# Zero products in the idle time of the TensorE queue, and a planner with another clock and fetch model: a fused delta-rule attention and two MLPs on one Trainium2 core

## The chip, the cores and the metric

The kernel runs on one core of one Trainium2 chip. The metric is the device time of one execution in microseconds (us), the median of several runs. Five queues matter: PE (TensorE), ACT (ScalarE), DVE (VectorE), POOL (GpSimd) and SP (which issues the DMAs). Each executes its own instructions in the order in which they were emitted and waits on semaphores for the others.

## What is computed

```python
k_n = k / (norm(k) + 1e-6)
for t in range(768):                       # 4 batches x 8 heads, head size 48
    y[t]  = q[t] @ state
    state = state + beta[t] * outer(k_n[t], v[t] - k_n[t] @ state)
x = y as [3072, 384]
x = ((x @ w_a) * (x @ w_b)) @ w_out        # hidden size 1536
h = x @ w_in                               # hidden size 2048
out = (max(h, 0) + alpha * min(h, 0)) @ w_out2
```

All tensors are float32.

## The kernel before

The sequence is cut into six pieces of 128 steps (`c = 0..5`), each of two halves of 64 (`j`). For a piece the kernel forms products of the keys with the keys and with the queries (`gram_keys`, `gram_queries`, PSUM tiles `g`), masks them (`ef` on DVE, `Z` on POOL), inverts the triangular 32x32 blocks by a chain of small DVE operations (`inverting`: pairs `itmp`, `inv`), transposes the result (`diagonal`: `hw`, `TT` on DVE), joins the blocks (`offdiag`: products `w`, ACT copies into `hw`, products `xx`, ACT copies into `TT`), and then walks through the two halves (`step`: products `rp`, `up`, `sp`, `yp`, with `v` and `SU` evicted between them). `columns` splits `yp` into the high and the low float32r half of `x`. All products of this part are fp32 with at most 128 columns, and the profile shows two PE instructions for each.

The MLPs use float32r products of 128x128 by 128x512, three for each fp32 product (high by high, low by high, high by low). The first MLP has, for a piece, 12 hidden blocks `m` of nine products `p` for `w_a`, nine `p` for `w_b` and nine `o` for `w_out`. Its weights come packed. `decode` unpacks each by ACT (`W`, `e`), DVE (two operations on `raw`) and POOL (`W`); `prepare` splits it into a ring `u` of four tiles `wu` by ACT and POOL. The order in which weights are prepared is fixed: `w_a` and `w_b` of block 0, of block 1, `w_out` of block 0, `w_a` and `w_b` of block 2, `w_out` of block 1, and so on. The second MLP (products `h` and `o`) follows when all six pieces are through the first.

"The front" is what comes ahead of the first `p` of piece 0. In it the core loads pieces 0 and 1 (called `L` and `N` in the code), does the whole attention of piece 0, and does `N`'s products of keys and queries and `N`'s inversion beside it. The inversions of `L` and `N` run in a PSUM tile `inv` of a pool `p0`, which also has the bank `g`. The bank for the products `o` comes from a pool that begins only when `p0` is no longer used (`Pool(rec, second, (p0,), 1, True)`), thus after `N`'s inversion and the two transposes that read it. The other PSUM banks of the front are rings by tag: `chain` (two banks: two of `L`'s query products, then `w`, `xx`, `rp`, ...), `ab` (two), `pre` (one).

Nothing of this is emitted in program order. A `Recorder` takes all operations down with what they depend on; `Recorder.link` adds the dependences that come from tiles sharing a place; `Schedule` groups consecutive small products into one task, gives each task a cost, computes its level (the longest chain of work behind it, in which the large products also follow one another), and `Schedule.run` plays the whole kernel through: always the engine that can begin first, and on it the ready task of the highest level. The order of the starts is the order of emission on each queue. In this play a product costs double while a small model of PE's clock says slow. The model of before starts fast, adds up PE's busy time in steps of fixed length, and switches by two shares, `RISE` and `KEEP_UP`.

Of the kernel before, what the change touches and what calls it, by code (L numbers as in the profile page):

```python
# [6 lines left out]
F32R = mybir.dt.float32r  # L7
# [11 lines left out]
class View:  # L19
# [3 lines left out]
    def __init__(s, tile, path, p, ix):  # L23
        s.tile, s.path, s.p, s.ix = tile, path, p, ix
# [101 lines left out]
PE_, ACT_, DVE_, POOL_, SP_ = range(5)  # L126


class Recorder:
# [35 lines left out]

    def link(s):

        for pool in s.pools:
            earlier = {n for p in pool.after for r in p.rooms for n in r.uses}
            rings = {}  # L170
            for room in sorted((r for r in pool.rooms if r.uses), key=lambda r: r.uses[0]):
                ring = rings.setdefault(room.kw.get("tag", id(room)), [])
                first = s.ops[room.uses[0]]
                for n in earlier:
                    first.before.setdefault(n, 0)
                k = room.kw.get("bufs", pool.bufs)
                if len(ring) >= k:
                    for n in ring[-k].uses:
                        first.before.setdefault(n, 0)
                if ring:  # L180
                    first.before.setdefault(ring[-1].uses[0], 1)
                for n in room.uses[1:]:
                    s.ops[n].before.setdefault(first.n, 1)
                ring.append(room)
        for op in s.ops:
            op.before.pop(op.n, None)
# [17 lines left out]
HOP, SAME = 0.15, 0.03  # L204
ENTER, LEAVE = 0.2, 0.19
SLACKS = (0.25, 0.15, 0.15, 0.3, 0.3)
WINDOW, RISE, KEEP_UP = 3.413, 0.93, 0.66


class Task:  # L210
# [4 lines left out]
def large(op):  # L215
    return op.name == "matmul" and op.dst.ix.size >= 256
# [6 lines left out]
class Schedule:  # L223

    def __init__(s, rec):
        s.tasks, s.of = [], {}
        for op in rec.ops:
            t = s.tasks[-1] if s.tasks else None
            if op.eng == PE_ and not large(op) and t and t.eng == PE_ and not t.large and t.ops[-1].n == op.n - 1:
                t.ops.append(op)  # L230
            else:
                t = Task()
                t.n, t.eng, t.ops, t.large = len(s.tasks), op.eng, [op], op.eng == PE_ and large(op)
                t.port, t.dma, t.after, t.rows = False, op.name == "dma_start", [], None
                s.tasks.append(t)
            s.of[op.n] = t.n
        for t in s.tasks:
            s.costs(t)
            t.before = {}
            for op in t.ops:  # L240
                for n, kind in op.before.items():
                    m = s.of[n]
                    if m != t.n:
                        t.before[m] = min(kind, t.before.get(m, 1))
            for m in t.before:
                s.tasks[m].after.append(t.n)

    def costs(s, t):
        op, k = t.ops[0], len(t.ops)
# [67 lines left out]
    def run(s, level):  # L317

        tasks = s.tasks
        waits = [len(t.before) for t in tasks]  # L320
        ready, start, end = ([0.0] * len(tasks) for _ in range(3))
        open_ = [[t.n for t in tasks if t.eng == e and not waits[t.n]] for e in range(5)]
        free, port, link, was = [0.0] * 5, 0.0, 0.0, False
        rows = [None] * 5
        landed, order = [], []
        clock = {"w": 0, "busy": 0.0, "fast": True}

        def fast(b):
            while (clock["w"] + 1) * WINDOW <= b:
                share = clock["busy"] / WINDOW  # L330
                clock["fast"] = share >= (KEEP_UP if clock["fast"] else RISE)
                clock["busy"], clock["w"] = max(0.0, clock["busy"] - WINDOW), clock["w"] + 1
                if clock["busy"] == 0 and (clock["w"] + 1) * WINDOW <= b:
                    clock["fast"] = False
            return clock["fast"]

        while len(order) < len(tasks):
            at, e = min((min(max(ready[n], free[e]) for n in open_[e]), e) for e in range(5) if open_[e])
            n = max((n for n in open_[e] if ready[n] <= at + SLACKS[e]), key=lambda n: (level[n], -n))
            open_[e].remove(n)  # L340
            t = tasks[n]
            order.append(n)
            b = max(ready[n], free[e])
            cost, lag = t.cost, t.lag
            if e in (ACT_, DVE_, POOL_):
                if rows[e] == t.rows:
                    b = max(ready[n], free[e] - (0.12 if e != DVE_ else 0.1))
                rows[e] = t.rows
            if t.port:
                wait = max(0.0, port - b - 0.1)  # L350
                port = b + wait + t.lag - 0.05
                cost, lag = cost + wait, lag + wait
            if e == PE_:
                if t.large == was:
                    b += ENTER if not t.large else LEAVE
                    clock["busy"] += 0.2
                was = not t.large
                if not fast(b):
                    cost *= 2
                    lag = lag + t.cost  # L360
                clock["busy"] += cost
            if t.dma:
                if e == SP_:
                    if len(landed) >= 8:
                        b = max(b, landed[-8])
                    landed.append(0)
                link = max(b + 1.5, link) + lag
                end[n] = link + 0.55
                if e == SP_:
                    landed[-1] = end[n]  # L370
            else:
                end[n] = b + lag
            start[n] = b
            free[e] = b + cost
            for m in t.after:
                u = tasks[m]
                if u.before[n]:
                    r = b + 1e-6
                elif u.eng == e == PE_:
                    r = b + cost  # L380
                else:
                    r = end[n] + (SAME if u.eng == e and not t.dma else HOP)
                ready[m] = max(ready[m], r)
                waits[m] -= 1
                if not waits[m]:
                    open_[u.eng].append(m)
        s.start, s.end = start, end
        return sorted(order, key=lambda n: (start[n], n))


B, H, S, D = 4, 8, 768, 48
# [57 lines left out]
def f32(ap):  # L449
    return ap.bitcast(F32)  # L450
# [415 lines left out]
def attn_moe_kernel(tc, kt, qt, kn, vn, beta, w_a, w_b, w_o, w_in, w_o2, alpha, out):  # L866
    nc = tc.nc
    with ExitStack() as ctx:
        ctx.enter_context(tc.manual_schedule(engines={getattr(mybir.EngineType, e) for e in ("PE", "Activation", "DVE", "Pool", "SP")}))
        rec = Recorder(nc)  # L870
        nc = rec

        def pool(name, stack=ctx, bufs=1, **k):
            p = Pool(rec, None, (), bufs, k.get("space") == PSUM)
            p.real = stack.enter_context(tc.tile_pool(name=name, bufs=bufs, **k))
            return p

        cp, wp, xp, gp = pool("const"), pool("wp"), pool("xp"), pool("gp", bufs=2)
# [12 lines left out]
        def bank(name, tag):  # L891
            return pools[tag].tile([128, 512], F32, tag=tag, name=name, bufs=BANKS[tag])
# [29 lines left out]
        now, until = 0.0, {ACT: 0.0, DVE: 0.0, POOL: 0.0, SP: 0.0}  # L922
# [182 lines left out]
        def finish(b):  # L1105
            for _ in b:
                pass
            background[:] = [x for x in background if x is not b]
# [13 lines left out]
        A.masks(L, 1, xroom(0, 1, [16, 64], F32, "mb1"))  # L1122
        A.scale_values(L, 0)
        A.clear()

        ef1 = wp.tile([128, 32, 64], F32, tag="late", name="ef1")
        for jg, tag in zip(HALF, ("ab", "ab", "g", "pre")):
# [12 lines left out]
        A.scale_values(L, 1)  # L1140
        norms = A.norms(N, ef1, late=True)
        next(norms)
        keys = [A.gram_keys(N, *jg, tag) for jg, tag in zip(HALF, ("g", "pre", "ab", "ab"))]
        finish(inv)
        finish(A.diagonal(L))
        finish(norms)
# [67 lines left out]
        free, spare = ["mb", "eu", "ef"], [f"w{n}" for n in range(6)]  # L1214
# [49 lines left out]
        now = 220.0  # L1264
# [15 lines left out]
        n = 0  # L1280
# [17 lines left out]
        for c in range(NSC):  # L1298
# [3 lines left out]
            if c > 0:  # L1302
                N = A.load(c + 1) if c + 1 < NSC else None
                if c == 1:
                    finish(inv)
                    diagonal = A.diagonal(L)
                    now = max(now, until[DVE])
# [9 lines left out]
                tag = "chain" if c == 1 else "pre"  # L1317
# [48 lines left out]
        def fetched(c):  # L1366

            fs = []
            for kk in range(KT):
                fs.append(wp.tile([128, 512], F32, tag=("w6", "w8", "w9")[kk], name="xf"))  # L1370
                nc.sync.dma_start(fs[kk], x2d[c][kk])
            return fs
# [56 lines left out]
        first = hidden2(0, xn)  # L1429
# [4 lines left out]
        for c in range(NSC):  # L1434
            xs = xn
            for m in range(M2):
                if m == XAT and c + 1 < NSC:
                    xf, xn = fetched(c + 1), []
                if c == m == 0:
                    g = first  # L1440
                elif c == NSC - 1 and m == M2 - 1:
                    g = hidden2(m, xs, 2, nc.vector)
                else:
                    g = hidden2(m, xs)
# [4 lines left out]
                if m == 0:  # L1449
                    o = [bank("o2", tag) for tag in OUT[c % 2]]  # L1450
# [1 line left out]
        down2(*todo)  # L1452
        rec.link()
        plan = Schedule(rec)
        rec.emit([op.n for n in plan.run(plan.levels()) for op in plan.tasks[n].ops])


def _layout(q, k, v, beta, moe_w_a, moe_w_b, moe_w_out, moe2_w_in, moe2_w_out, moe2_alpha):
# [74 lines left out]
```

## Time and profile before

| | |
|---|---|
| three runs | 1020.69, 1021.53, 1021.54 us; median 1021.53 us |
| profiled execution, first to last instruction (span) | 1019.1 us |
| what lies around the span, against the median | 2.4 us |
| PE busy | 977.5 us (96%), 9950 products |
| DVE, POOL, ACT busy | 610.0, 574.7, 477.4 us |
| PE busy from 100 to 200 us | 99.93 of 100 us |
| PE busy in the first 80 us | 45.07 of 80 us |
| granted clock of PE, mean of the span | 0.977 |

The time of the profiled execution itself isn't listed beside its span; the table sets the span against the median of the three runs. [...] In the profile PE is busy nearly without a break from the first `p` at 81.04 us to the end of the last product at about 1013.8 us; before that its work is small, with gaps, and the clock rises and falls. So the page as a whole says that PE is the bound, and the front has to be read for itself, engine by engine.

### The profile page before, as it was taken

What the parts mean: (1) busy time and instruction counts of PE and PEld (TensorE: products, weight loads), DVE (VectorE), ACT (ScalarE), POOL (GpSimd) and SP (SyncE); (2) the same over time, 40 slices, a digit from 0 to 9 for tenths busy, and PEclk for the clock granted to TensorE, in tenths of its full rate; (3) what the DMA queues carried; (4) which work ended last, traced back from release to release, by engine and by line L of the source; (5) the groups of instructions that cost most, each with busy time, mean ns of one, the idle gap of its engine ahead of it and who ended that gap; (6) DMA issues with size and microseconds to landing.
All of it is one profiled execution on the core that took longest, in us unless ns stands there. A gap on an engine that the chain in (4) does not pass through costs nothing.

```text
span 1019.1 us, 23984 instructions
## 1 busy us (share of the span) xinstructions
PE 977.5 (96%) x9950; PEld 805.1 (79%) x9950; DVE 610.0 (60%) x1232; ACT 477.4 (47%) x955; POOL 574.7 (56%) x512
## 2 busy tenths in 40 slices
PE   6279999999999999999999999999999999999998
PEld 5267877888888788878878888888888888888886
DVE  6999667854783587368648899543343443433333
ACT  5477875565547455645578886122121221211211
POOL 7668998667567566755546996333333333333332
PEclk9569999999999999999999999999999999999999
DMA  9624434101300220000025541101020020000000
GB/s 248 190 81 126 138 115 132 40 2 50 110 1 8 74 79 1 18 19 32 17 64 171 178 146 50 32 19 44 1 63 0 1 63 1 32 1 1 32 0 32
DMA packets 26940, 61.41 MB, mean 60 GB/s; under 512 B 4304, under 2 KB 8912, under 8 KB 26832
## 3 DMA queue, kind: packets, MB, share of 16 engines
q1 hardware_dynamic: 26400, 59.50, 19.3%
q8 instruction: 78, 1.28, 0.5%
q10 hardware_dynamic: 432, 0.39, 0.1%
q14 instruction: 30, 0.25, 0.1%
HBM read 50.44 MB, written 9.44 MB: 59 GB/s over the span
## 4 chain that ended last, share of the span: by engine, by line
PE 91%; DVE 5%; ACT 1%; issue 1%; DMA 1%; SPq 0%; DVEq 0%; POOL 0%; ACTq 0%
PE o L201 34%; PE p L201 29%; PE h L201 19%; PE up L201 2%; PE yp L201 2%; PE g L201 2%; DVE itmp L201 1%; DVE inv L201 1%; PE rp L201 1%; PE sp L201 1%; DMA k<-in_kn_dram 1%; PE xx L201 1%; PE w L201 1%; DVE raw L201 1%; DVE ef L201 0%
## 5 line engine op out<-in xcount | busy, mean ns | idle before, releaser
L201 PE MATMUL p<-x,wu 128*128 128x512 f32 x1296 | 318.0, 394 | 1.4 <-DVE x L201 0.7
L201 PEld LDWEIGHTS p<-x,wu 128*128 128x128 f32 x1296 | 240.2, 188 | 56.2 <-issue 2.4
L201 POOL TENSOR_TENSOR g<-neg,g 128x512 fp32r<-128x512 f32 x95 | 124.3, 1308 | 256.2 <-ACT g L201 255.6
L201 POOL TENSOR_TENSOR wu<-W,wu 128x384 fp32r<-128x384 f32 x195 | 200.3, 1033 | 110.6 <-ACT wu L201 109.0
L201 PE MATMUL h<-x,v 128*128 128x512 f32 x864 | 211.4, 389 | 0.0
L201 PE MATMUL o<-g,v 128*128 128x512 f32 x870 | 211.4, 388 | 0.0
L201 DVE TENSOR_SCALAR neg<-h,al 128x512 f32<-128x512 f32 (+1 forms) x97 | 72.2, 745 | 218.3 <-PE h L201 218.3
L201 ACT CAST g<-neg 128x512 fp32r<-128x512 f32 (+1 forms) x97 | 59.7, 616 | 298.8 <-DVE neg L201 277.3
L201 PEld LDWEIGHTS o<-g,v 128*128 128x128 f32 x870 | 162.5, 188 | 33.4
L201 PEld LDWEIGHTS h<-x,v 128*128 128x128 f32 x864 | 162.2, 188 | 33.7
L201 PE MATMUL o<-g,wu 128*128 128x512 f32 x648 | 165.5, 394 | 0.5 <-DVE TT L201 0.5
L201 ACT CAST wu<-W 128x384 fp32r<-128x384 f32 x216 | 109.9, 513 | 78.7 <-PE p L201 38.2
L201 PEld LDWEIGHTS o<-g,wu 128*128 128x128 f32 x648 | 120.0, 188 | 27.1 <-issue 0.9
L201 POOL TENSOR_TENSOR g<-a,g 128x512 fp32r<-128x512 f32 x71 | 93.3, 1314 | 30.3 <-ACT g L201 30.1
L201 PE MATMUL g<-Z 48*64 48x64 f32 (+1 forms) x1024 | 66.4, 275 | 27.9 <-DVE ef L201 17.9
L201 DVE TENSOR_TENSOR a<-p,a 128x512 f32<-128x512 f32 x72 | 49.3, 685 | 49.8 <-PE p L201 22.4
L201 DVE TENSOR_TENSOR inv<-inv,itmp 128x240 f32<-128x240 f32 (+23 forms) x236 | 69.9, 296 | 10.4 <-ACT eu L201 2.8
L201 PEld LDWEIGHTS g<-Z 48*64 48x64 f32 x1024 | 50.6, 160 | 28.9 <-DVE ef L201 18.2
L201 DVE SCALAR_TENSOR_TENSOR neg<-h,neg 128x512 f32<-128x512 f32 (+1 forms) x97 | 66.5, 686 | 3.3
L201 ACT COPY a<-p 128x512 f32<-128x512 f32 x72 | 42.2, 586 | 44.7 <-PE p L201 41.6
L201 ACT CAST g<-a 128x512 fp32r<-128x512 f32 x72 | 44.7, 620 | 22.5 <-DVE a L201 22.0
L201 POOL TENSOR_TENSOR f<-f,v 128x384 int32<-128x384 int32 x32 | 38.2, 1205 | 6.6 <-DVE v L201 4.0
(87 smaller groups left out, 948.5 us busy)
## 6 DMA issues: line engine op xcount, KB each, us to landing
v<-in_w_o_dram SPq DMA_DIRECT2D x16, 384.0 KB, 3.2
v<-in_w_in_dram SPq DMA_DIRECT2D x16, 384.0 KB, 3.7
k<-in_kn_dram SPq DMA_DIRECT2D x6, 768.0 KB, 4.6
Z<-in_kt_dram SPq DMA_DIRECT2D x24, 192.0 KB, 4.4
Z<-in_qt_dram SPq DMA_DIRECT2D x24, 192.0 KB, 4.0
raw<-in_w_a_dram SPq DMA_DIRECT2D x12, 384.0 KB, 4.0
v<-in_vn_dram SPq DMA_DIRECT2D x12, 384.0 KB, 3.3
raw<-in_w_b_dram SPq DMA_DIRECT2D x12, 384.0 KB, 4.4
```

Of the source, the lines that this page charges most:

```text
L201: getattr(s.engines[op.eng], op.name)(*(real(x) for x in op.a), **{w: real(x) for w, x in op.k.items()})
```

## The change

- A tile `still` of 128x512 zeros is made by a memset on DVE. It uses the ring `a`, which the first MLP uses later.
- `spins` records 120 products of `still` with itself (128x128 by 128x512, float32r) into a bank, under a tag. There are two such groups: `early`, into the ring `chain` between `L`'s second query product and `w`; and `late`, into the bank `g` behind `N`'s first key product. Nothing reads what they write.
- `Schedule` takes tagged operations out of the tasks. In `run`, ahead of each PE task until the first large product, `spin` fills the time from when PE is free until `REST` (0.5 us) before the task's planned start with as many of these products as fit, at 0.227 us each or double while the clock model says slow. `early` stops when the first task that needs its bank (`w`) has begun, and gives it at least one product; `late` goes on until the first large product. Products that don't fit are not emitted.
- The clock model starts slow, keeps a list of PE's busy stretches instead of one sum, counts the zero products as busy, and has other constants.
- A model of PE's instruction stream is new: a stock of instructions, then pieces of 256, each asked for when the piece before it is begun and there 3.5 us later, or 6.6 us while data is being loaded. A PE task is planned longer by the wait for a piece.
- The order in which the tasks are emitted follows from this play, so it may differ from that of before on every queue, SP's and POOL's included. No data product, DMA or vector operation is added or left out but the memset and the zero products.

```diff
+        s.next = {}
...
+                    s.next.setdefault(ring[-1].uses[0], []).append(first.n)
...
-WINDOW, RISE, KEEP_UP = 3.413, 0.93, 0.66
+REST, SPIN, SPINS = 0.5, 0.227, 120
+CHUNK, STOCK, FETCH_IDLE, FETCH_BUSY = 256, 446, 3.5, 6.6
+WINDOW, RISE, KEEP_UP = 3.413, 0.98, 0.65
...
+            if op.tag is not None:
+                spins.setdefault(op.tag, []).append(op)
+                continue
...
+        s.spins = []
+        for ops in spins.values():
+            ends = [s.of[n] for n in rec.next.get(ops[0].n, ())]
+            s.spins.append((ops, [s.of[n] for n in ops[0].before], ends))
...
-        clock = {"w": 0, "busy": 0.0, "fast": True}
+        spins, filled = [0] * len(s.spins), []
+        chunk, spans = {"at": 0, "next": 0.0}, []
+        clock = {"w": 0, "fast": False}
...
+        def ask(b):
+            chunk["next"] = b + (FETCH_BUSY if link > b + 1 else FETCH_IDLE)
+
+        def fetched(b, cost, n):
+            at, late = chunk["at"], 0.0
+            for x in range(at, at + n):
+                if x == STOCK - CHUNK:
+                    ask(b)
+                if x >= STOCK and (x - STOCK) % CHUNK == 0:
+                    now = b + late + cost * (x - at) / n
+                    late += max(0.0, chunk["next"] - now)
+                    ask(max(now, chunk["next"]))
+            chunk["at"] = at + n
+            return late
+
+        def spin(b, t):
+            for g, (ops, before, ends) in enumerate(s.spins):
+                if all(end[n] for n in before) and not any(end[n] for n in ends):
+                    at = max(free[PE_], max(end[n] for n in before) + HOP)
+                    while spins[g] < len(ops):
+                        each = SPIN if fast(at) else 2 * SPIN
+                        if at + each > b - REST and (spins[g] or t.n not in ends):
+                            break
+                        filled.append((at, 0, ops[spins[g]]))
+                        spins[g] += 1
+                        spans.append((at, at + each))
+                        fetched(at, each, 2)
+                        at += each
+                    b = max(b, at)
+            return b
...
             if e == PE_:
+                if not done:
+                    b = spin(b, t)
+                done = done or t.large
...
+                late = fetched(b, cost, 2 if t.large else 4 * len(t.ops))
+                cost, lag = cost + late, lag + late
+                spans.append((b, b + cost))
...
+        still = gp.tile([128, 512], F32R, tag="a", name="still")
+        nc.vector.memset(f32(still), 0.0)
+
+        def spins(name, tag):
+            rec.now_tag, o = name, bank(name, tag)
+            for _ in range(SPINS):
+                nc.tensor.matmul(o, still[:, 0:128], still, start=True, stop=True)
+            rec.now_tag = None
...
+        spins("early", "chain")
         keys = [A.gram_keys(N, *jg, tag) for jg, tag in zip(HALF, ("g", "pre", "ab", "ab"))]
+        spins("late", "g")
```

## Rows read from the trace of the kernel before

**Rows 1.** The page: each engine's busy time, share of the span, instructions.
```profile
PE 977.5 (96%) x9950; PEld 805.1 (79%) x9950; DVE 610.0 (60%) x1232; ACT 477.4 (47%) x955; POOL 574.7 (56%) x512
```

**Rows 2.** Busy time by stretch: length, PE, PEld, DVE, ACT, POOL, clock, DMA, GB/s.
```profile
40.00:60.00 20.00, 11.08 (x384) 10.23 (x384) 18.71 (x45) 14.98 (x30) 6.54 (x6) 0.50 0.10 33
60.00:80.00 20.00, 17.03 (x569) 16.23 (x571) 18.84 (x46) 12.98 (x30) 15.05 (x14) 0.72 0.38 102
```

**Rows 3.** Single microseconds, PE alone: length, busy (products), clock, DMA, GB/s.
```profile
12.00:13.00 1.00, 1.00 (x24) 1.00 1.06 212
16.00:17.00 1.00, 1.00 (x42) 1.00 1.00 205
46.00:47.00 1.00, 1.00 (x25) 0.50 0.00 0
64.00:65.00 1.00, 1.00 (x34) 0.75 0.10 16
71.00:72.00 1.00, 0.00 (x0) 0.66 0.28 52
```

**Rows 4.** PE in order of time, the front: start, length, what [idle before].
```profile
26.88 1.27 PE L201 MATMUL g<-Z 48*64 48x64 f32 x35 [1.33 <-issue]
44.84 3.75 PE L201 MATMUL g<-Z 48*64 48x64 f32 x64 [16.68 <-DVE ef L201]
48.63 1.54 PE L201 MATMUL w<-hw,ef 32*32 32x32 f32 x128
...
54.72 1.92 PE L201 MATMUL xx<-TT,hw 32*32 32x32 f32 x128 [0.60 <-ACT hw L201]
60.45 3.65 PE L201 MATMUL up<-v,TT 64*64 64x48 f32 x64 [3.81 <-ACT TT L201]
...
72.09 3.65 PE L201 MATMUL up<-v,TT 64*64 64x48 f32 x64 [1.80 <-DVE v L201]
...
76.95 2.54 PE L201 MATMUL yp<-Z,SU 112*32 112x64 f32 x128
```

**Rows 5.** PE in order of time, from the first large product on.
```profile
81.04 6.38 PE L201 MATMUL p<-x,wu 128*128 128x512 f32 x27 [0.70 <-DVE x L201]
87.94 3.58 PE L201 MATMUL p<-x,wu 128*128 128x512 f32 x13 [0.52 <-DVE a L201]
92.04 2.35 PE L201 MATMUL o<-g,wu 128*128 128x512 f32 x9 [0.52 <-DVE TT L201]
...
107.70 1.29 PE L201 MATMUL w<-hw,ef 32*32 32x32 f32 x128
...
119.25 4.24 PE L201 MATMUL p<-x,wu 128*128 128x512 f32 x18
...
125.36 4.56 PE L201 MATMUL p<-x,wu 128*128 128x512 f32 x18
```

**Rows 6.** The tile up on PE at clock 1.00, half of it, beside other products.
```profile
139.00:141.00 2.00, 1.13 (x32) 1.00 0.38 119
```

**Rows 7.** ACT in order of time: start, length, what [idle before].
```profile
52.14 1.02 ACT L201 COPY inv<-eu 128x1024 f32<-128x1024 f32 x1 [0.84 <-DVE eu L201]
```

**Rows 8.** DVE in order of time: start, length, what [idle before].
```profile
7.04 1.75 DVE L201 TENSOR_REDUCE ss<-ef 128x32 f32<-128x1536 f32 x1 [1.64 <-ACT ef L201]
...
66.74 2.27 DVE L201 TENSOR_TENSOR SU<-SU,sp 48x384 f32<-48x384 f32 x4
...
71.49 1.71 DVE L201 TENSOR_TENSOR v<-rp,v 128x384 f32<-128x384 f32 x3
...
89.98 2.00 DVE L201 STREAM_TRANSPOSE TT<-inv 128x1024 f32<-128x1024 f32 x1
```

**Rows 9.** POOL in order of time, two waits of its unpacking of weights.
```profile
83.06 1.02 POOL L201 TENSOR_TENSOR W<-W,raw 128x384 int32<-128x384 int32 x1 [1.33 <-DVE raw L201]
85.36 1.02 POOL L201 TENSOR_TENSOR W<-W,raw 128x384 int32<-128x384 int32 x1 [1.28 <-DVE raw L201]
```

**Rows 10.** A stretch behind the front, columns as in the second group.
```profile
100.00:110.00 10.00, 10.00 (x168) 8.18 (x167) 7.39 (x15) 7.50 (x17) 10.00 (x11) 1.00 0.14 45
```

More of the change, by code (lines that the diff above doesn't have):

```diff
@@ L225, in __init__ @@
     def __init__(s, rec):
-        s.tasks, s.of = [], {}
+        s.tasks, s.of, spins = [], {}, {}
         for op in rec.ops:
+            if op.tag is not None:
+                spins.setdefault(op.tag, []).append(op)
+                continue
             t = s.tasks[-1] if s.tasks else None
@@ L241, in __init__ @@
                 for n, kind in op.before.items():
-                    m = s.of[n]
+                    m = s.of.get(n, t.n)
                     if m != t.n:
@@ L322, in run @@
         open_ = [[t.n for t in tasks if t.eng == e and not waits[t.n]] for e in range(5)]
-        free, port, link, was = [0.0] * 5, 0.0, 0.0, False
+        free, port, link, was, done = [0.0] * 5, 0.0, 0.0, False, False
         rows = [None] * 5
         landed, order = [], []
-        clock = {"w": 0, "busy": 0.0, "fast": True}
+        spins, filled = [0] * len(s.spins), []
+        chunk, spans = {"at": 0, "next": 0.0}, []
+        clock = {"w": 0, "fast": False}
         def fast(b):
             while (clock["w"] + 1) * WINDOW <= b:
[L330 to L334, printed above, removed]
-            return clock["fast"]
+                lo, hi = clock["w"] * WINDOW, (clock["w"] + 1) * WINDOW
+                busy = sum(min(y, hi) - max(x, lo) for x, y in spans if y > lo and x < hi)
+                spans[:] = [(x, y) for x, y in spans if y > hi]
+                clock["fast"] = busy >= WINDOW * (KEEP_UP if clock["fast"] else RISE)
+                clock["w"] += 1
+            return clock["fast"]
@@ L353, in run @@
             if e == PE_:
+                if not done:
+                    b = spin(b, t)
+                done = done or t.large
                 if t.large == was:
                     b += ENTER if not t.large else LEAVE
-                    clock["busy"] += 0.2
+                    spans.append((b - 0.2, b))
                 was = not t.large
                 if not fast(b):
-                    cost *= 2
-                    lag = lag + t.cost
-                clock["busy"] += cost
+                    cost += t.cost
+                    lag += t.cost
+                late = fetched(b, cost, 2 if t.large else 4 * len(t.ops))
+                cost, lag = cost + late, lag + late
+                spans.append((b, b + cost))
             if t.dma:
@@ L387, in run @@
         s.start, s.end = start, end
-        return sorted(order, key=lambda n: (start[n], n))
+        ops = [(start[n], n, op) for n in order for op in tasks[n].ops] + filled
+        return [op.n for _, _, op in sorted(ops, key=lambda x: x[:2])]
 B, H, S, D = 4, 8, 768, 48
@@ L1454, in attn_moe_kernel @@
         plan = Schedule(rec)
-        rec.emit([op.n for n in plan.run(plan.levels()) for op in plan.tasks[n].ops])
+        rec.emit(plan.run(plan.levels()))
 def _layout(q, k, v, beta, moe_w_a, moe_w_b, moe_w_out, moe2_w_in, moe2_w_out, moe2_alpha):
```

## The prediction

> **What bounds the kernel now.** I read the page first: PE is busy 96% of the span [rows 1], and behind the front it has almost no idle time. So the end is the time at which PE's large products begin, plus a fixed sum of PE work, plus the little that PE idles afterwards. The change adds no data work and takes none away; only the front, up to the first `p` at 81.04 us [rows 5], can give time back.
>
> The front has three layers. The busy times by stretch show that between 40 and 80 us no engine is near its limit but DVE: 18.71 and 18.84 of 20 us, while PE stands at 11.08 and 17.03 [rows 2]. DVE goes through `L`'s inversion, then `N`'s, and nothing in the change shortens that. The single microseconds show PE's clock. [...] PE had been idle for 16.68 us until 44.84 us [rows 4], and the clock is low from then until it rises inside 64 to 65 us; it falls again inside 71 to 72 us, after a microsecond with no product, and is low for `up` of the second half [rows 3, 4]. The third layer is PE in order of time: `w`, `xx`, `up`, `up` and `yp` of piece 0 stand on the chain that ends in `x`, and most of them run at the low clock [rows 4].
>
> **The zero products: number and price.** 18 large products take 4.24 us [rows 5], so one is at most 0.236 us at the high clock, about 0.47 us at the low one. The gap of 16.68 us less the planned rest of 0.5 us holds about 70 of them, and the later gaps of 0.60, 3.81 and 1.80 us [rows 4] some 20 together. They run in PE's idle time, so they cost nothing as long as they end before the product behind them is released. PE's queue is in order: whatever they overrun delays `g`, then `w`, and so the whole of `L`'s chain. Their cover at 44.84 us is good: at the high clock the 64 `g` products need about 1.5 us (64 at 42 in a microsecond [rows 3]) instead of 3.75, and `w` behind them isn't released before 48.63 us, so 2 us of overrun cost nothing. The memset of `still` has a third of the elements of the DVE reduction that takes 1.75 us, so I bound it by 0.6 us; DVE waits 1.64 us ahead of that reduction [rows 8], so I cost it at nothing, and at 0.6 us if it lands elsewhere.
>
> **What the high clock gives on the chain to x.** Term by term:
> - `w`: 1.54 us becomes 1.29, its length at clock 1.00 [rows 4, 5]. ACT, which empties it, then waits 0.84 us for DVE in the middle of its copies [rows 7], so this is hidden. 0; 0.25 without that cover.
> - `xx`: 1.92 us becomes about 1.3, as `w`. ACT is copying other blocks of `TT` until 57.7 us anyway. 0; 0.6 without that cover.
> - First `up`: 3.65 us. Half of it takes 1.13 us at clock 1.00 beside other products [rows 6], so the whole is at most 2.26; at 42 in a microsecond it is 1.5. I take 1.8, nearest to the rows of like products alone. ACT can take its second half 1.25 us earlier. `sp` behind it gains 0.3. DVE reaches `SU` at 66.74 us [rows 8], behind an unpacking step that waited for ACT; 0.45 us of gain if that order stays, 1.5 if `SU` is put first. I take 1.2, since the planner will see `SU` ready at the earlier time and its level is the higher.
> - `v` on DVE: `rp` ends about 70.3 us, DVE takes `v` at 71.49 [rows 8], behind steps of `N`'s inversion. Between 0 and 1.0; I take 0.5.
> - Second `up`: 3.65 us [rows 4], of which its second half must wait for the third `v` operation, about 73.2 us. 1.5, between 1.4 and 1.85.
> - `yp`: 2.54 us [rows 4] for products that are partly at the high clock already. 0.55, between 0.5 and 0.6.
> The sum is 1.2 + 0.5 + 1.5 + 0.55 = 3.75 us, between 2.35 and 4.95. The first `p` would start at about 77.3 us.
>
> **What is late next.** Two things stand behind. First, the first `o` waits for `N`'s last transpose on DVE: 89.98 plus 2.00, and `o` starts at 92.04 us [rows 8, 5]. DVE is full up to there, so this point doesn't move with PE. With four tiles `wu` and the order of preparation given, PE can do six groups of nine `p`, 54 products, before it; it had done 27 + 13 = 40 [rows 5]. So 14 products, 14 x 0.227 = 3.2 us (0.227 is the 6.38 us of 27 products less the tail of the last), are what it can get ahead, and `N`'s `w`, 1.29 us, is a filler once its transpose is there. The cap is about 4.4 us, above the 3.75. I take 0.6 us off for one more `a` product on DVE ahead of the transposes and for PE's waits there. Second, POOL: from 100 to 110 us it is busy all the time [rows 10], and at 125.36 us 18 `p` take 4.56 us instead of 4.24 [rows 5], so the split weights come just in time there. PE that is 3 us ahead needs them 3 us earlier. POOL has 1.33 + 1.28 us of waiting at 82 to 86 us [rows 9], which it can fill with splits as the tiles `wu` come free earlier, and PE has attention products of piece 1 to put between. I take 0.3 us off.
>
> **The planner's own order.** The changed clock and fetch model may reorder any queue: ACT's and DVE's vector work, POOL's unpacking and the DMA issues of SP. No row shows that order; its price is bounded by the misplacements that the order of before shows: ACT's 0.84 us [rows 7], DVE's 1.0 us ahead of `v`. I take 0, with 1 us on either side. On instruction fetches: the trace has one stall of PE that nothing else explains, 1.33 us ahead of 26.88 us [rows 4], and it delayed nothing, as PE idles right after. [...]
>
> Result: 3.75 - 0.6 - 0.3 = 2.85 us. The span was 1019.1 us and 2.4 us lie around it, which makes the median of 1021.53; what lies around stays. 1021.53 - 2.85 = 1018.7 us.
>
> **Rivals.**
> 1. POOL takes it back. If PE's earlier start finds no earlier weights between 110 and 150 us, PE waits there for the 3 us that it was ahead. For: POOL at 10.00 of 10 us and the slow 18 products [rows 10, 5]. Against: the POOL waits that can be filled, and fillers. It gives 1020.5 to 1021.5; with it I count the case that the gaps as planned are too short to hold the clock up, so that nothing changes. 0.31.
> 2. Zero products in the way: slower. If a share s of the 70 runs at the low clock while the plan has them at the high one, PE is late at 44.84 us by s x 70 x 0.236 = 16.5 s. The cover there is about 2 us, the rest 0.5, and the gain to lose 2.85; so it turns at s of about 0.3, and it is slower by 2 us from about 0.45. If zeros don't raise the clock at all, s is 1: some 14 us late at `w`, and the kernel ends near 1033. Against it: 18 large products in 4.24 us [rows 5] have the length of the high clock, so products of this shape hold it once it is there; no row shows products of zeros. I give it 0.13, most of that close behind the point where it decides, near 1024.
> [...]
>
> **How the numbers follow.** The forecast with its bounds, 1016.1 to 1019.4, has 0.56; rival 1 has 0.31 within 0.2% (2 us, about what a measurement of this kernel can tell from no change); rival 2 has 0.13. The range reaches from the largest sum, cut to 4.4 us by the cap and with 1 us for a better order, 1021.53 - 5.4 = 1016.1, to the end of rival 1 with half of the order's bound, 1022.0; it leaves out rival 2 and a little below.
>
> **What would show it.** Right: clock 1.00 from 28 us on through the front; `up` at about 1.8 us both times; the first `p` near 77; `o` still near 92, with some 54 products ahead of it; no new gaps of PE between 110 and 150 us. Wrong: a low clock in 45 to 80 us; `g` later than 46.5 us or `w` later than 49 with zero products right ahead of it; a first `o` that moved; PE waiting for `wu` at 110 to 150 us. The sum fails first where I let the planner put `SU` and `v` ahead, and at the cap by DVE.

## The result and the profile after

The changed kernel takes 1032.04 us (median of 4 runs, 1030.97 to 1033.77) against 1021.53 us: 1.0106 times the time before, interval 1.0091 to 1.0120. It is 10.5 us slower, where 1018.7 us was forecast. The profiled span grew from 1019.1 to 1029.4 us.

The page of the kernel after, first part, columns as in [rows 1]:

```profile
PE 1004.4 (98%) x10079; PEld 824.1 (80%) x10079; DVE 611.1 (59%) x1233; ACT 477.9 (46%) x955; POOL 574.7 (56%) x512
```

129 products more than before, all of them zeros: PE is busier and the kernel slower. PE's share is no measure here, since the filling counts as work.

The kernel after, PE in order of time (start, length, what, [idle before]); between 49.44 and 53.43 us single `early` and `late` products alternate, 18 in all:

```profile
19.92 6.52 PE L203 MATMUL g<-Z 48*64 48x64 f32 x155 [0.23 <-DMA Z<-in_qt_dram]
28.05 1.27 PE L203 MATMUL g<-Z 48*64 48x64 f32 x35 [1.61 <-issue]
29.26 17.11 PE L203 MATMUL early<-still 128*128 128x512 f32 x74
...
47.43 2.08 PE L203 MATMUL g<-Z 48*64 48x64 f32 x64
49.44 0.50 PE L203 MATMUL early<-still 128*128 128x512 f32 x1
...
53.75 1.29 PE L203 MATMUL w<-hw,ef 32*32 32x32 f32 x128
...
62.11 0.28 PE L203 MATMUL xx<-TT,hw 32*32 32x32 f32 x13 [1.68 <-issue]
62.33 3.24 PE L203 MATMUL late<-still 128*128 128x512 f32 x13
65.50 2.07 PE L203 MATMUL up<-v,TT 64*64 64x48 f32 x64
...
89.01 10.58 PE L203 MATMUL p<-x,wu 128*128 128x512 f32 x39 [1.99 <-DVE x L203]
99.72 2.32 PE L203 MATMUL o<-g,wu 128*128 128x512 f32 x9
```

The same engine steps stood at 26.88, 44.84, 48.63, 60.45, 81.04 and 92.04 us [rows 4, 5]. `w` comes 5.12 us late, right behind products of zeros. The kernel after, DVE and ACT in order of time:

```profile
5.45 0.48 DVE L203 MEMSET still<- 128x512 f32 x1 [0.15 <-issue]
7.58 1.75 DVE L203 TENSOR_REDUCE ss<-ef 128x32 f32<-128x1536 f32 x1 [1.64 <-ACT ef L203]
...
47.07 1.97 DVE L203 STREAM_TRANSPOSE hw<-inv 128x1024 f32<-128x1024 f32 x1
...
58.24 0.20 DVE L203 TENSOR_TENSOR itmp<-inv,eu 128x30 f32<-128x30 f32 x1 [4.46 <-ACT inv L203]
...
71.81 0.56 DVE L203 TENSOR_SCALAR raw<-e 128x384 int32<-128x384 int32 x1 [0.98 <-ACT e L203]
72.40 2.27 DVE L203 TENSOR_TENSOR SU<-SU,sp 48x384 f32<-48x384 f32 x4
...
88.12 1.08 DVE L203 TENSOR_TENSOR x<-yp,x 128x256 fp32r<-128x256 f32 x3
```
```profile
55.06 2.23 ACT L203 COPY hw<-w 32x256 f32<-32x256 f32 x6 [4.04 <-PE w L203]
57.21 1.00 ACT L203 COPY inv<-eu 128x1024 f32<-128x1024 f32 x1
```

DVE had `hw` ready at 47.07 + 1.97 = 49.04 us; nothing but PE's queue holds `w` until 53.75. ACT stands 4.04 us for `w`, and the copy `inv`, with which `N`'s inversion begins, is queued behind `w`'s copies on ACT. So DVE, the bound of the front, stands idle for 4.46 us ahead of 58.24. Everything behind that, down to `SU` (72.40 for 66.74), keeps the delay. With 0.52 us by which `hw` is late already and 0.95 us more of waiting for ACT behind 58.24, DVE is 5.94 us late at 85.75. The other 2.0 us of the first `p` are four steps of `N`'s inversion and two unpacking steps, which the new order puts ahead of `x`. DVE, the kernel before, then after:

```profile
79.81 0.35 DVE L201 TENSOR_TENSOR inv<-inv,itmp 128x184 f32<-128x184 f32 x1
80.13 0.76 DVE L201 TENSOR_TENSOR x<-yp,x 128x256 fp32r<-128x256 f32 x2
```
```profile
85.75 0.35 DVE L203 TENSOR_TENSOR inv<-inv,itmp 128x184 f32<-128x184 f32 x1
...
94.94 0.69 DVE L203 TENSOR_TENSOR a<-p,a 128x512 f32<-128x512 f32 x1 [1.73 <-PE p L203]
```

Behind the first `p` DVE stands still for another 1.73 us, now for PE: one `a` is queued ahead of `N`'s transposes. PE had come out of 1.99 idle us with the clock at 0.50 from 89 to 92 us, so that the 39 `p` take 10.58 us, about 1.4 more than at the rate of 18 in 4.24 [rows 5]. They end at 99.59 us, `N`'s last transpose at 99.58; the first `o` is 7.68 us late by either.

The kernel after from 40 to 60 us, columns as in [rows 2]:

```profile
40.00:60.00 20.00, 19.32 (x400) 16.01 (x399) 14.78 (x33) 11.13 (x21) 7.54 (x6) 1.00 0.14 43
```

The clock is at 1.00, as intended, and DVE works 14.78 us of the 20 in which it had worked 18.71. That is the loss in one pair of numbers.

### The profile page after: what moved, and what is told of

It reads as the page before. It is cut to its first block, busy times and chain, and to the rows that moved or that the text cites. A ratio compares the mean times of both kernels' runs of the same rounds, so it can differ in the third digit from the quotient of the medians.

```text
span 1029.4 us, 24250 instructions
## 1 busy us (share of the span) xinstructions
PE 1004.4 (98%) x10079; PEld 824.1 (80%) x10079; DVE 611.1 (59%) x1233; ACT 477.9 (46%) x955; POOL 574.7 (56%) x512
## 3 DMA queue, kind: packets, MB, share of 16 engines
q8 instruction: 79, 1.29, 0.5%
## 4 chain that ended last, share of the span: by engine, by line
PE 90%; POOL 3%; DMA 2%; issue 2%; DVE 1%; ACT 1%; SPq 0%; DVEq 0%; POOLq 0%; ACTq 0%
PE o L203 33%; PE p L203 27%; PE h L203 19%; PE g L203 3%; PE yp L203 2%; PE early L203 2%; DMA Z<-in_qt_dram 2%; PE up L203 1%; PE rp L203 1%; POOL W L203 1%; PE sp L203 1%; POOL wu L203 1%; PE xx L203 1%; PE late L203 1%; PE w L203 1%
## 5 line engine op out<-in xcount | busy, mean ns | idle before, releaser
L203 POOL TENSOR_TENSOR wu<-W,wu 128x384 fp32r<-128x384 f32 x195 | 200.4, 1033 | 108.7 <-ACT wu L203 105.4
L203 DVE TENSOR_SCALAR neg<-h,al 128x512 f32<-128x512 f32 (+1 forms) x97 | 72.3, 745 | 218.4 <-PE h L203 218.4
L203 PE MATMUL g<-Z 48*64 48x64 f32 (+1 forms) x1024 | 64.1, 266 | 12.1 <-DMA Z<-in_kt_dram 7.2
L203 PEld LDWEIGHTS g<-Z 48*64 48x64 f32 x1024 | 48.5, 151 | 13.4 <-DMA Z<-in_kt_dram 7.4
L203 DVE TENSOR_TENSOR itmp<-inv,eu 128x240 f32<-128x240 f32 (+28 forms) x120 | 37.2, 310 | 9.1 <-ACT inv L203 5.3
```

The lines of the kernel that those rows point to most:

```text
L203: getattr(s.engines[op.eng], op.name)(*(real(x) for x in op.a), **{w: real(x) for w, x in op.k.items()})
```

## The experiments

Each result stands beside runs of the kernel before on the same chip. The landmarks are from one profiled execution each; for e1, e4, e9 and e10 it lies 1.4 to 2.8 us above the median of its runs, for e14 2.3 us below:

| kernel | median us | ratio, interval | first `up` | first `p` | first `o` | `up` to `o` | span |
|---|---|---|---|---|---|---|---|
| before | 1021.53 | | 60.45 | 81.04 | 92.04 | 31.59 | 1019.1 |
| after | 1032.04 | 1.0106 (1.0091, 1.0120) | 65.50 | 89.01 | 99.72 | 34.22 | 1029.4 |
| e1, one fill | 1029.33 | 1.0075 (1.0060, 1.0090) | 65.88 | 88.46 | 98.32 | 32.44 | 1028.7 |
| e3, zeros, old models | 1027.59 | 1.0055 (1.0039, 1.0072) | 66.89 | 87.87 | 98.94 | 32.05 | 1025.4 |
| e10, e3 with one fill | 1026.60 | 1.0050 (1.0032, 1.0068) | 66.91 | 87.87 | 98.95 | 32.04 | 1027.2 |
| e6b, zeros out of the way | 1020.83 | 0.9996 (0.9986, 1.0005) | 60.47 | 81.59 | 92.07 | 31.60 | 1018.7 |
| e2, new models, no zeros | 1026.44 | 1.0046 (1.0031, 1.0061) | 60.40 | 85.09 | 96.00 | 35.60 | 1025.5 |
| e5, clock model alone | 1024.53 | 1.0031 (1.0020, 1.0042) | 60.43 | 82.01 | 93.94 | 33.51 | 1023.4 |
| e9, fetch model alone | 1036.65 | 1.0142 (1.0126, 1.0159) | 61.96 | 87.76 | 101.82 | 39.86 | 1036.3 |
| e12, memset alone | 1022.68 | 1.0013 (1.0004, 1.0023) | 61.00 | 81.96 | 92.96 | 31.96 | 1019.9 |
| e4, memset on POOL | 1032.97 | 1.0112 (1.0093, 1.0131) | 71.28 | 95.45 | 104.67 | 33.39 | 1033.8 |
| e13, `SU` first | 1028.09 | 1.0057 (1.0037, 1.0077) | 60.45 | 81.08 | 93.15 | 32.70 | 1026.4 |
| e14, e13 with e6b's zeros | 1027.35 | 1.0056 (1.0037, 1.0074) | 60.49 | 80.77 | 92.93 | 32.44 | 1023.1 |

**The two halves of the change.** e2 keeps the planner's new models and leaves out the zero products and the memset; e3 keeps the zero products and the memset and plans with the clock model of before and no fetch model. Both edits are against the changed kernel.

```diff
 # e2
-        still = gp.tile([128, 512], F32R, tag="a", name="still")
-        nc.vector.memset(f32(still), 0.0)
 ...
-        spins("early", "chain")
 ...
-        spins("late", "g")
 # e3
-WINDOW, RISE, KEEP_UP = 3.413, 0.98, 0.65
+WINDOW, RISE, KEEP_UP = 3.413, 0.93, 0.66
 ...
-                late = fetched(b, cost, 2 if t.large else 4 * len(t.ops))
-                cost, lag = cost + late, lag + late
-                spans.append((b, b + cost))
+                clock["busy"] += cost
```

> The planner's new clock and fetch models alone: no zero products, no memset of zeros, the banks as before. Theory A: the order itself costs little, 1020.5 to 1023. Rival B: 1027 or more. Rival C: near 1021, with at most the one issue wait of 1.33 us that the kernel before has.

> The zero products as in the change, double filling included, but the order planned with the clock model of before and without the fetch model. Theory A: w is as late as in the changed kernel, near 53.7 us, and the time is 1028 to 1032. Rival B: the time returns to 1021 or 1022. Rival C: 1030 to 1032, with the issue waits of the changed kernel.

Each half is slower alone: e2 by 4.7 us (1026.44 - 1021.76), e3 by 5.8. The memset is in e3 alone. That the two losses add up to 10.5 doesn't show that they don't act on each other (e3 has 144 zero products, the changed kernel 129); but neither half is innocent, and neither is a gain spoiled by the other.

They lose in different places. e3 loses all ahead of the first `up`, which comes 6.44 us late, and keeps that to the end (span +6.3). e2 has `up` on time and loses behind it. The kernel e2, PE, then DVE:

```profile
73.54 3.56 PE L203 MATMUL up<-v,TT 64*64 64x48 f32 x64 [3.30 <-DVE v L203]
...
85.09 11.07 PE L203 MATMUL p<-x,wu 128*128 128x512 f32 x36 [3.83 <-DVE x L203]
```
```profile
72.94 1.70 DVE L203 TENSOR_TENSOR v<-rp,v 128x384 f32<-128x384 f32 x3
```

`v` starts at 72.94 us (before: 71.49 [rows 8]) though `rp` is done at 69.11 + 1.14 = 70.25: the new order has put steps of `N`'s inversion and an unpacking step between. The second `x` is late too, and PE, having idled 3.83 us, starts its 36 `p` at the low clock (0.50 from 85 to 90 us): 11.07 us, where 27 of them take 6.38 [rows 5].

**Is it the clock model or the fetch model?** e5 is e2 without the fetch model; e9 is e2 with the clock model of before.

```diff
 # e5
-                late = fetched(b, cost, 2 if t.large else 4 * len(t.ops))
-                cost, lag = cost + late, lag + late
 # e9
-WINDOW, RISE, KEEP_UP = 3.413, 0.98, 0.65
+WINDOW, RISE, KEEP_UP = 3.413, 0.93, 0.66
 ...
-        clock = {"w": 0, "fast": False}
+        clock = {"w": 0, "busy": 0.0, "fast": True}
```

> The order planned with the new clock model but without the fetch model, no zero products: the kernel of e2_no_zeros without its fetch model. Theory B1 (the fetch model plans stalls of PE that the chip doesn't have, so the evictions v and x are queued too late on DVE and ACT; it is what costs the 4.7 us of e2): 1020.5 to 1023, with PE's waits for v and x back near 1.8 and 0.7 us. Rival B2 (the clock model costs them): 1025 to 1027.

> The kernel before with the fetch model in its planner alone, its clock model kept, no zero products. Theory B1: v and x are late on DVE as in e2_no_zeros, first p at 84 to 87 us, 1025 to 1029. Rival B2: 1020.5 to 1023.

Both cost: +2.9 us and +15.0 us against 1021.62, and together only +4.7. So they don't add; a planner that is told another price reorders everything, and the loss can't be read off the prices put in. The kernel e9, PE:

```profile
76.10 3.65 PE L203 MATMUL up<-v,TT 64*64 64x48 f32 x64 [3.77 <-DVE v L203]
...
87.76 6.40 PE L203 MATMUL p<-x,wu 128*128 128x512 f32 x27 [3.07 <-DVE x L203]
97.81 4.21 PE L203 MATMUL p<-x,wu 128*128 128x512 f32 x9 [3.65 <-DVE a L203]
```

All three waits are for DVE, which had other work ahead in its queue: `rp` for that `v` was done at 72.3 us. That fits an order planned for a PE that the fetch model makes late; the plan itself isn't on record. e5 shows the same at smaller size (waits of 1.92 for `x`, 1.29 and 1.74 for `a`).

**Why are the zeros in the way?** In `spin` the fill of the second group begins again at `free[PE_]`, where the first group's began. While both groups are open (from `N`'s first key mask to `w`), one gap is planned full twice, and PE runs both. e1 mends that in the changed kernel, e10 in e3:

```diff
+            at = free[PE_]
             for g, (ops, before, ends) in enumerate(s.spins):
                 if all(end[n] for n in before) and not any(end[n] for n in ends):
-                    at = max(free[PE_], max(end[n] for n in before) + HOP)
+                    at = max(at, max(end[n] for n in before) + HOP)
```

> The changed kernel, but the second group of zero products is planned behind the first one's instead of into the same gap again. Theory A (the gap ahead of w is filled twice: 19 zero products, alternately early and late, from 49.44 to 53.75 us, while hw is ready at 49.04): w starts near 49.2 us, some 4.5 us sooner, with at most 10 zero products ahead of it, DVE's wait of 4.46 us goes, and the time falls by 4 to 6 us to 1026 to 1028. Rival B (the new order of the planner is what costs): w is sooner but the time stays within 2 us of 1032. Rival C (instruction fetches, as the zero products use up the stock): the issue waits of 1.61, 0.68, 1.68 and 0.53 us stay and the time stays above 1029.

> The kernel of e3_zeros_old_plan (1027.6 us) with the second group of zero products planned behind the first instead of into the same gap. Theory A: w at 49.5 to 52 us instead of 54.2, and 1022.5 to 1025; what is left above the kernel before is the memset (0.54 us) and the early group that starts late behind a fetch stall and so ends late. If the double filling isn't what costs in e3, it stays at 1026.5 to 1028.

e1 wins back 2.7 us of the 10.5, e10 at most 1.0 of e3's 5.8 (the intervals of that pair overlap). The double filling is real, and not the main thing. (In e1's profiled execution `hw` itself was ready only at 49.53 + 2.08 = 51.61 us, for a reason given in the last section, so its `w` at 52.17 says little about the filling.) The kernel e10 shows what is left, PE, then ACT:

```profile
21.18 7.86 PE L203 MATMUL g<-Z 48*64 48x64 f32 x155 [0.28 <-DMA Z<-in_qt_dram]
29.70 1.27 PE L203 MATMUL g<-Z 48*64 48x64 f32 x35 [0.66 <-issue]
30.90 17.07 PE L203 MATMUL early<-still 128*128 128x512 f32 x74
47.90 2.08 PE L203 MATMUL g<-Z 48*64 48x64 f32 x64
49.92 2.34 PE L203 MATMUL early<-still 128*128 128x512 f32 x9
52.18 1.40 PE L203 MATMUL w<-hw,ef 32*32 32x32 f32 x128
...
61.44 5.54 PE L203 MATMUL late<-still 128*128 128x512 f32 x16
66.91 2.07 PE L203 MATMUL up<-v,TT 64*64 64x48 f32 x64
```
```profile
61.61 3.00 ACT L203 COPY TT<-xx 32x256 f32<-32x256 f32 x8 [1.38 <-PE xx L203]
...
68.09 1.94 ACT L203 COPY SU<-up 64x384 f32<-64x384 f32 x4 [2.88 <-PE up L203]
```

A block of zeros is a count, fixed when the kernel is built. 74 products take 17.07 us here and 17.11 in after, and here they start at 30.90 us, where PE came free at 28.15 before [rows 4]. An empty gap would have swallowed the 2.75 us; the full one passes them on, and `g` is 3.06 us late, of which `ef` on DVE, late by 0.93 us (43.84 for 42.91), would explain no more than that. The nine behind `g` and the 16 behind `xx` do the same: these 16 run in part at the low clock (0.50 from 63 to 65 us; 5.54 us, where 18 large products take 4.24 [rows 5]), and `up` waits for them until 66.91 us, though ACT had `TT` done at 64.61.

**Can they be put where they harm nothing?** e6b takes e10's fill, lets the first group stop 7.0 us ahead of the planned start, the second 1.2 us, and gives the memset the level 0, so that it comes behind `one`.

```diff
+            if t.ops[0].dst is not None and t.ops[0].dst.tile.kw.get("name") == "still":
+                level[n] = 0.0
 ...
+                    rest = 7.0 if ends else 1.2
 ...
-                        if at + each > b - REST and (spins[g] or t.n not in ends):
+                        if at + each > b - rest and (spins[g] or t.n not in ends):
```

> The order of the kernel before, with zero products that keep out of the way: the two groups end to end, the early group ends 7 us ahead of the planned start of its successor, the late group 1.2 us, and the memset comes behind the one of the tile one. If the high clock in the front is worth what the forecast said: first p at 77 to 79 us and 1017.5 to 1019.5. Rival (DVE's order decides: SU stands behind unpacking steps and the inversion of N, whatever PE does): up at about 2.1 us instead of 3.65 where zeros precede it, but SU on DVE still near 66.7 us, first p at 80 to 81.5, 1020.5 to 1022. Third (zero products in the way is all that costs in e10, so that it is gone here): at most 1022; if they cost something else besides: above 1022.5.

The kernel e6b, PE:

```profile
28.46 10.49 PE L203 MATMUL early<-still 128*128 128x512 f32 x45
44.84 3.75 PE L203 MATMUL g<-Z 48*64 48x64 f32 x64 [5.88 <-DVE ef L203]
...
60.47 3.65 PE L203 MATMUL up<-v,TT 64*64 64x48 f32 x64 [1.02 <-issue]
```

1020.83 us, 0.9996 (0.9986 to 1.0005) of before: no harm, and no gain, for after 5.88 idle us the clock is low again when `g` starts (0.50 from 44 to 60 us), and `up` takes its 3.65 us as ever. With these rests, what is far enough away to be harmless is too far to hold the clock; rests between 0.5 and 7.0 us for the first group weren't measured. It also shows that 54 zero products by themselves cost nothing.

**What is the high clock worth where it does hold?** e3 answers: from 25 us on its products run at the rate of the high level (42 products of queries from 25 to 26 us), and no change of the clock is on record (1.000 as the mean of the span). The kernel e3, PE, then DVE:

```profile
66.89 2.07 PE L203 MATMUL up<-v,TT 64*64 64x48 f32 x64
...
87.87 6.38 PE L203 MATMUL p<-x,wu 128*128 128x512 f32 x27 [0.71 <-DVE x L203]
...
98.94 2.31 PE L203 MATMUL o<-g,wu 128*128 128x512 f32 x9 [0.60 <-DVE TT L203]
```
```profile
73.20 0.56 DVE L203 TENSOR_SCALAR raw<-e 128x384 int32<-128x384 int32 x1 [1.94 <-ACT e L203]
73.79 2.27 DVE L203 TENSOR_TENSOR SU<-SU,sp 48x384 f32<-48x384 f32 x4
```
```profile
72.64 0.53 ACT L203 ACTIVATE e<-raw 128x384 f32<-128x384 f32 x1
```

`up` takes 2.07 us for 3.65, and yet from `up` to the first `p` it is 20.98 us, where before it was 81.04 - 60.45 = 20.59. `sp` is done by 71.2 us; DVE stands still for 1.94 us all the same, since its next instruction is the unpacking of `e`, and `SU` is queued behind it, in the same place as before [rows 8]. ACT (the last line) brings that `e` only at 72.64 us, behind three copies `Z`, a `wu` and a `W`; in before `e` stood ahead of the last `Z`, `wu` and `W`, at 65.61. So e3's order isn't that of before, though its models are, and in this order PE's speed isn't on the path: the queues of ACT and DVE are.

The changed planner of e1 has `e` right behind the copies into `SU`, and there the high clock does reach DVE. The kernel e1, DVE:

```profile
70.04 2.27 DVE L203 TENSOR_TENSOR SU<-SU,sp 48x384 f32<-48x384 f32 x4
```

That is 4.16 us behind `up` (65.88), where before it was 66.74 - 60.45 = 6.29. The 2.1 us are lost again further on: PE stands still for 1.62 us within `yp`, with "issue" as the releaser, and `v` begins at 76.75 us, 1.66 us behind the end of `rp`.

**And if `SU` is put first?** e13 changes nothing in the kernel before but that the planner takes `SU` of the first half, and `v` and `x` of piece 0, ahead of all else that is ready on DVE; e14 adds e6b's zeros to that.

```diff
+        front = min(t.n for t in tasks if t.large)
+        named = [(t.n, t.ops[0].dst.tile.kw.get("name")) for t in tasks[:front] if t.eng == DVE_]
+        first = [n for n, name in named if name == "SU"][:4] + [n for n, name in named if name in ("v", "x")]
+        urgent = [100.0 * (t.n in first) for t in tasks]
 ...
-            n = max((n for n in open_[e] if ready[n] <= at + SLACKS[e]), key=lambda n: (level[n], -n))
+            n = max((n for n in open_[e] if ready[n] <= at + SLACKS[e]), key=lambda n: (level[n] + urgent[n], -n))
```

> The kernel before, without zero products, but its planner puts SU (first half), v and x of piece 0 ahead of everything else on DVE, as the prediction had assumed that it would. The inversion of N is then later by what is put ahead. If the chain to x decides: first p at 79 to 80.5 us and 1019.5 to 1021. If the inversion of N decides through the first o: first p earlier but o later than 92.04 us, 1021 to 1024.

> e13_su_first and the zero products of e6b_zeros_out_of_the_way together. If the high clock pays once DVE's order lets it through: 1.5 to 3 us below e13_su_first. If it doesn't even then: within 1 us of e13_su_first.

6.7 us slower (1028.09 for 1021.41), and with the zeros 5.9; the two can't be told apart. The kernel e13, DVE, then PE by stretch (columns as in [rows 2]):

```profile
66.72 1.12 DVE L201 TENSOR_TENSOR SU<-SU,sp 48x384 f32<-48x384 f32 x2 [0.18 <-PE sp L201]
71.52 1.70 DVE L201 TENSOR_TENSOR v<-rp,v 128x384 f32<-128x384 f32 x3
...
91.15 1.95 DVE L201 STREAM_TRANSPOSE TT<-inv 128x1024 f32<-128x1024 f32 x1
```
```profile
150.00:200.00 50.00, 46.73 (x702) 36.54 (x701) 36.74 (x99) 28.28 (x61) 36.54 (x32) 0.97 0.33 97
```

`SU` ends 1.2 us earlier, but `v` starts at 71.52 us against 71.49, with inversion and unpacking steps still ahead of it though `rp` is done at 68.61 + 1.15 = 69.76. The first `p` stands at 81.08 against 81.04, and `N`'s transpose is 1.17 us later, so the first `o` is 1.1 us later. PE then misses over 3 us more at 150 to 200 us, where POOL's share fell too; why the queues that follow fit so much worse wasn't followed up. So e13 shows no gain from `SU` first at the low clock (its first `up` takes 3.65 us). e14 doesn't test it at the high one: its zeros keep as far away as e6b's, and its first `up` takes 3.65 us like that of before. The kernel e14, PE:

```profile
60.49 3.65 PE L203 MATMUL up<-v,TT 64*64 64x48 f32 x64 [1.06 <-issue]
```

An order made for the high clock, with the clock high, was never measured.

**The memset.** e12 adds only the tile and its memset to the kernel before; e4 moves it, in the changed kernel, to POOL.

```diff
 # e12
+        still = gp.tile([128, 512], F32R, tag="a", name="still")
+        nc.vector.memset(f32(still), 0.0)
 # e4
-        nc.vector.memset(f32(still), 0.0)
+        nc.gpsimd.memset(f32(still), 0.0)
```

> The kernel before with the memset of 128x512 zeros on DVE at the place where the change has it, and nothing else. If its 0.5 us reach the end through the tile one, ACT's first square and the chain of the inversion: 1022.0 to 1022.3. If hidden: 1021.6.

> The changed kernel with the memset of the zeros on POOL instead of DVE. In the changed kernel it takes 0.48 us on DVE ahead of the memset of the tile one, for which ACT's first square waits, and everything behind starts 0.54 us later than before. If that delay reaches the end, the time falls by about 0.5 us to 1031.5; if it is hidden, it stays at 1032.0. Theories A, B and C all expect no more than this.

e12 costs 1.3 us (1022.68 for 1021.41; by its interval 0.4 to 2.3). In it, as in the kernel after, the 0.48 us of the memset stand ahead of `one`, for which ACT's first activation waits: `ss` moves from 7.04 to 7.58 us with the whole front behind it. e4 shows no gain (1032.97 us, its interval overlaps that of after): on POOL it comes only at 8.30 us, and a stall of PE with "issue" as the releaser is 3.69 us in its profile, so that run tells nothing about the memset itself. e6b holds the memset behind `one`, has `ss` at 7.04, and shows no loss.

**What the expectations missed.** e2, e3 and e5 lie between the ranges put down for them, e4, e9, e12 and e13 above all of theirs, e9 and e13 by over 4 us. No theory here foresaw the size of what a reordering costs.

## Why the prediction was wrong

- **"They cost nothing as long as they end before the product behind them is released"** failed, and with it the 2 us of cover. The reading allowed for one group per gap and for an end that is a matter of the clock. But 18 products, 4.2 us, stand between `g` and `w`, twice the nine that one fill leaves there (e10), and the 74 ahead of `g` began 1.1 us later than the gap of before had opened. So `w` came 5.12 us late.
- **Rival 2 had the side, but not the mechanism.** It let zeros run at the low clock; its 1033 us for zeros that don't raise the clock lies near the result by chance. The 74 took 17.11 us, 0.231 each: all at the high level, s = 0. The clock was at 1.00 through 40 to 75 us. (In e1 and e4 a share of the block did run at 0.50: 19.11 us for 76 and 18.92 for 74.) What made them late is that a counted block can't shrink, and its start moves. That belonged among the rivals, and wasn't there.
- **The 3.75 us of the high clock** didn't come. `up` did become 2.07 us (1.8 taken), and `sp` shorter; `up` to `p` was 20.98 us in e3, where the clock was high, for 20.59, and 23.51 in after. The failed step is the one in which `SU` was put first "since its level is the higher": `SU` stays behind an unpacking step in after and e3, for a reason that isn't on record. Where that step comes sooner (e1), 2.1 us arrive at `SU` and are gone at `v`; where `SU` is forced first at the low clock (e13), the gain ends at `v` too. That no order could keep it isn't shown.
- **The planner's order, 0 with 1 us on either side,** was mis-sized: +4.7 us in e2, which has no memset, +2.9 in e5, +15.0 in e9. Misplacements in the order of before bound nothing, because the new order isn't near the old one.
- **The memset, 0 with a bound of 0.6:** the bound by a longer reduction held for its length (0.48), but it landed ahead of the instruction that ACT waits for: 0.54 us at `ss`, 0.8 of span, 1.3 in the runs (e12). DVE's wait of 1.64 us ahead of `ss` was no cover: that wait is for ACT, and ACT waits for DVE's `one`.
- **What held, in part:** DVE bounds the front, and the first `o` comes 0.05 to 0.15 us behind `N`'s last transpose in before, e3 and e13, where PE waits for it. That is how 4.46 us of DVE's idle time reach the end. But DVE wasn't "full up to there": in after it waited for ACT and for PE's `p` besides, and PE had no idle time left ahead of `o`, with 39 `p` done and not 54.
- **Rival 1** (POOL takes it back) isn't where the loss lies: at 100 to 150 us PE is busy 49.59 us of 50.

Of the 10.3 us of span, 7.7 are there at the first `o`. The rest is PE's idle time further on (0.4 us more than before at 100 to 150 us, 0.3 at 150 to 200, 0.7 at 200 to 300), one `p` fewer ahead of `o`, and about 1 us that wasn't followed.

## What to carry to other kernels

Filling an in-order queue with a counted block turns its slack into a duty (in after `w` started 4.71 us behind its ready `hw`): fill only up to where the latest likely start still ends before the next real instruction, and look first whether the engine that would be sped up is awaited at all, by the idle time and the order of the engines behind it. A planner's model is a change of its own, to be timed alone before anything is built on it; its effect on the time here couldn't be read off the prices put in. An "idle" engine that waits for another one isn't cover if that other one waits for it.

## What the runs showed of the hardware

**Products of zeros held the clock in after.** From 24 to 75 us it shows 1.00 throughout; in before it was 0.50 from 40 to 60 us [rows 2]. Not everywhere, though: in e10 it was at 0.50 from 63 to 65 us with zero products running.

**Ahead of the first recorded change the printed clock and the rate of products disagree.** In after the page counts 25 small products in a microsecond at 0.50 (21 to 23 us) and 42 at 1.00 (25 to 26 us), but 24 beside a printed 1.00 at 12 to 13 us; the first change on record comes inside 17 to 18 us. In before it is alike at 12 us [rows 3].

**The clock rose at another point from profile to profile.** The same 155 products of queries took 6.28 us in the profile of before, 6.52 in after, 7.86 in e10, and in e1:

```profile
18.05 4.73 PE L203 MATMUL g<-Z 48*64 48x64 f32 x155 [0.38 <-DMA Z<-in_qt_dram]
```

In e10 the microseconds from 23 to 28 us hold 24 or 25 of them at 0.50, in after those from 24 to 26 us 41 and 42 at 1.00. The block of zeros behind them began at 26.83 us in e1, 29.26 in after and 30.90 in e10, with stalls of 0.66 to 2.84 us ahead of it in this, too. Each of these profiles is of another kernel, and what sets the point isn't shown. The four runs of e10 are 4.4 us apart, ten of before on the same chip 1.5; whether this comes from the clock isn't shown.

**Stalls of PE with "issue" as the releaser are more, and some are larger, than the one seen before.** 1.61, 0.68, 1.68 and 0.53 us in after, 2.84 in e1, 3.69 in e4, and 3.91 in e9, which has no zeros; before had 1.33 [rows 4]. In the front they stand always ahead of small products or within them; in ten profiles one stands ahead of the same last 35 products of queries (0.40 us in e6b to 3.91 in e9). In after ACT waits 0.85 us for `xx` behind the stall of 1.68. That they are instruction fetches, as the prediction and the expectations of e1 and e10 read them, isn't shown, nor are the pieces and the times that the fetch model plans with.

**A small DVE instruction beside a POOL operation.** The scaling `r` takes 0.18 us in after and 2.66 in e1, while POOL ran a product of two tensors on `Z` and then one on `v`, which ended at 22.02 us, as `r` did at 22.06; DVE, in e1:

```profile
19.40 2.66 DVE L203 TENSOR_SCALAR r<-r 128x32 f32<-128x32 f32 x1 [0.69 <-POOL r L203]
```

It set `L`'s chain back by 2.5 us in that execution, which is in e1's landmarks. No run here tells its cause.
